# Half of the column table computed and the rest mirrored on Pool, the leftover products of four row tiles put together, and the row statistics of a spectral block moved ahead

## The chip, the core and the metric

The kernel runs on one core of one Trainium2 chip. The metric is the device time of one execution in microseconds (us). A core has five engines with an instruction queue each: TensorE (PE, matrix products; PEld is its weight load), VectorE (DVE), ScalarE (ACT), GpSimd (POOL), and SyncE (SP), which here only issues DMAs. Each queue runs in program order; engines wait for one another by semaphores. Matrix products are written to PSUM, everything else lies in SBUF, in tiles of 128 partitions.

## What is computed

The input x has 2048 rows of 576 numbers in bf16. The first block adds a spectral filter of the normalised rows, the second a gated feed-forward part:

```python
def _A_ref(x, w_r, w_i):
    B, S, D = x.shape
    X = (lambda x, axes=(-2,-1): jnp.fft.rfft2(x.astype(jnp.float32), axes=axes))(x, axes=(-2, -1))
    W = w_r + 1j * w_i
    X = X * W
    y = (lambda x, s, axes=(-2,-1): jnp.fft.irfft2(x, s=s, axes=axes).astype(jnp.bfloat16))(X, (S, D), axes=(-2, -1))
    return y
def _B_ref(x, w_gate, w_up, w_down):
    return (_gelu(x @ w_gate) * (x @ w_up)) @ w_down
x = A_x
h = x + _A_ref(_layernorm(x, axis=-1), A_w_r, A_w_i)
h2 = h + _B_ref(_layernorm(h, axis=-1), B_w_gate, B_w_up, B_w_down)
```

The transform runs over 2048 rows and 576 columns; of the columns 289 frequencies are kept (J, padded to JP = 290). The gate and up weights are 576 x 4608, the down weight 4608 x 576.

## The kernel before

All transforms are matrix products with tables of sines and cosines. Row p * 16 + h of x lies in partition p, so there are sixteen row tiles h of 128 rows each. The program order of every engine is written out by hand (a manual schedule): what stands first in the code is first in that engine's queue.

**First stage** (lines 81 to 451). x comes in six DMAs, then the first halves of the filter WR and WI (line 154). POOL writes index patterns (`iota`, line 172) and the products `kd` from which the column phases come (lines 198 and 199). The first factor of the row transform, the table F16, comes from a sine on ACT (`fs`, line 209) times a mask (`row_table`, line 272). For each row tile the statistics are made either on DVE (`sd`: two `bn_stats` of half a row and one `bn_aggr`, lines 116 to 118; the even tiles and tile 15) or on ACT (`ln_act`, line 123: two passes with an accumulator, the other tiles, finished by `ln_fin` on POOL, lines 127 and 128). POOL then makes 1/sqrt of four tiles at once (`ln_rstd`, lines 132 and 133). DVE normalises each tile into xn (line 136), and PE multiplies it by F16: `row16` (line 288) takes the columns 0 to 255 and 288 to 543 of a tile in four products (line 298, PSUM tile f2t, two row tiles in one), `row16_rest` (line 308) the leftover 64-column pieces in two small ones (line 311, PSUM tile f4, four row tiles in one). Before some tiles `fill` (line 283) gives PE products that nobody reads. `evict` (line 319) and `evict4` (line 327) copy these results to Bt in SBUF, on ACT but for the last f4, which DVE copies. All PSUM tiles here come from one ring of four buffers (`two`, line 66), so the fifth tile waits for the release of the first.

Besides, this stage makes the tables of the later stages. The column table DT (three tiles of 128 columns of x by 2 parities a by cosine or sine r by 145 frequencies) comes from `phases` (line 266, DVE), `drop_sign` and two sines on ACT (`col_sin`, line 346). DF is a copy of a part of DT with zeros elsewhere (lines 387, 429, 430), and DQ a rearrangement of it, which thirteen DMAs on SP make (line 421). The row twiddles TF, nine frequencies k by (minus sine, cosine, sine) by 128, come from `angle_a`, `angle_b`, `angle_c` on DVE (lines 234 to 250), `sine` and `cosine` on ACT and `minus_sine` on DVE (line 258). They are made in two portions, `first` (the first two k in the order of use, 1 and 2) and `rest` (the other seven). `turn_tf` (line 261) makes the transposed copy TI of each portion with one transposing DMA on SP. G16 is a transposed F16 for the way back (line 437 on PE, line 445 on ACT). The second halves of WR and WI are mirrored rows, fetched by two indirect DMAs on POOL (line 381) and put in place by two DMAs on SP (line 411).

SP's queue in this part is: x, WR and WI, their second halves, `turn_tf(first)`, the thirteen DQ copies, `turn_tf(rest)`, then the first weights of the feed-forward part (`load_gu`, line 145, and line 693).

**Frequency stage** (lines 465 to 718). For each k in the order 1, 2, ..., 7, 0, spread over rounds i of one loop (line 668): `f2` multiplies Bt by the column table for k and k + 8 (line 479; `f2_out`, line 490, evicts), `f3` combines them with TF (lines 496 and 497), `sum_of` (line 529) and `wmul` (lines 547 to 571) on DVE form sums and multiply by the filter into Zt, and `i3` goes back over the rows with TI (line 587, one round later; k = 1 is turned in round 3, k = 3 in round 5). Then `inv_cols` (line 638) goes back over the columns with DQ, and `add_rows` (line 770) finishes the first block with G16.

**Feed-forward stage** (from line 850): products with the gate and up weights (line 898), gelu on ACT (line 906), the product on DVE (line 907), and the down product (line 941) with the sums and stores.

The functions that the change touches, with the numbers of the profile:

Of the kernel before, what the change touches and what calls it, by code (L numbers as in the profile page):

```python
# [20 lines left out]
P = 128  # L21
S = 2048
H = 16
D = 576
# [7 lines left out]
NDT = 5  # L32
JW = 58
# [8 lines left out]
def kernel_body(  # L42
# [143 lines left out]
    iota(q16[:], [[16, P]])  # L186
# [4 lines left out]
    iJ = tmp("iJ", [P, JP], FP32)  # L191
# [3 lines left out]
    pd, kd = tmp("pd", [P, 3, JP], FP32), tmp("kd", [P, 3, JP], FP32)  # L195
# [5 lines left out]
    iota(rev[:], [[0, 1]], 2 * P - 1, -2)  # L201

# [9 lines left out]
    ia, s2a, s2p = tmp("ia", [P, 1]), tmp("s2a", [P, 1], FP32), tmp("s2p", [P, 1], FP32)  # L212
    V.tensor_scalar(ia[:], ip[:], 7, None, op0=ALU.bitwise_and)
    V.tensor_scalar(s2a[:], ia[:], 127.0 / 8.0, None, op0=ALU.mult)
    V.scalar_tensor_tensor(s2p[:], ip[:], 0.125, s2a[:], op0=ALU.mult, op1=ALU.add)
    ks = tmp("ks", [P, 9], FP32)
    V.tensor_scalar(ks[:], kv[:], s2p[:, 0:1], None, op0=ALU.mult)
    V.tensor_scalar(iu[:], iu[:], 7, None, op0=ALU.bitwise_and)
    mask = tmp("mask", [P, P], FP32)
    V.tensor_scalar(mask[:], iu[:].rearrange("p c l -> p (c l)"), 0.0, None, op0=ALU.is_equal)  # L220
# [24 lines left out]
    def angle_b(sl):  # L245
        V.tensor_scalar(pr[:, sl], pr[:, sl], 2047, None, op0=ALU.bitwise_and)
        V.tensor_scalar(ab[:, sl], pr[:, sl], -1024.0, None, op0=ALU.add)
# [24 lines left out]
    def row_table():  # L272
        V.tensor_tensor(
            F16[:, 0:2, :],
            fs[:].unsqueeze(1).to_broadcast([P, 2, P]),
            mask[:].unsqueeze(1).to_broadcast([P, 2, P]),
            ALU.mult,
        )
        V.tensor_scalar(F16[:, 2, :], F16[:, 0, :], -1.0, None, op0=ALU.mult)
# [8 lines left out]
    def row16(h):  # L288
        if h % 2 == 0 or h == H - 1:
            ps_f[h] = two("f2t")  # L290
        if h % 4 == 0:
            ps_f["f4", h] = two("f4")
        f2t, b = (ps_f[h], 0) if h in ps_f else (ps_f[h - 1], 1)
        fill(f2t[:, b, :], {0: 14, 8: 8, 12: 5}.get(h, 0))
# [10 lines left out]
        if h < 12:  # L305
            row16_rest(h)
# [12 lines left out]
    def evict(*hs):  # L319
        for h in hs:  # L320
            n = 1 if h >= H - 2 else 2
            A.copy(  # L322
# [9 lines left out]

    def sd(*hs):
        for h in hs:
            ln_dve(mv, h)
# [6 lines left out]
    wm = [tmp(n, [P, 8 * J], BF16) for n in ("wm_r", "wm_i")]  # L342
    xn_pool = tc.tile_pool(name="xn", bufs=1, side="right")
    xn = xn_pool.__enter__().tile([P, H, D], BF16, name="xn")

    def col_sin(r, src, bias):
# [4 lines left out]
            bias=bias[:],  # L351
            scale=-2.0 * PI / D,
        )

    first, rest = slice(0, 2), slice(2, 9)
    ln_act(1)
    ln_act(3)
# [662 lines left out]
```

## Time and profile before

| | us |
|---|---|
| time, median of 3 runs (lowest, highest) | 497.41 (497.33, 497.72) |
| the profiled execution's own time | 497.44 |
| its span, first to last instruction | 495.7 |
| PE busy | 487.6 |
| first stage, to the first product of line 479 | 25.2 |
| first product of the feed-forward stage, line 898 | 68.1 |

The 1.7 us between the span and the time of the profiled execution lie outside its first and last instruction. A row of a timeline reads: start, length, engine, line, operation, output <- inputs with their shapes, count, and in brackets the idle time ahead of it and what ended it. Several instructions of one kind are merged into one row. The chain of waits is followed back from the last instruction; its rows give start, length, and engine, tile and line. SPq is SP's queue, with the time that issuing a DMA took. In the DMA view "under 512 B" counts the packets below that size.

### The profile page before, as it was taken

Reading aid. Unit: us, or ns where it says so; the run is one execution under the profiler, and the core shown is the slowest. Engines: PE = TensorE matmul, PEld = TensorE weight load, DVE = VectorE, ACT = ScalarE, POOL = GpSimd, SP = SyncE. Lnnn points to the kernel's source line nnn. Section 1 sums busy time; section 2 is a strip of 40 time slices with the busy share of each in tenths; the row PEclk is TensorE's granted clock in tenths of the full one; section 3 lists DMA queues with packets and bytes.
Section 4 is the critical chain, followed back from the end, with each engine's and each line's share of the span. In section 5 each row is a group of like instructions: output and inputs, shape, how many; then the busy total and the mean of one; then the engine's idle time right before and its main releaser. Section 6 shows DMA issues by size and latency. Waiting matters only on the chain.

```text
span 495.7 us, 12763 instructions
## 1 busy us (share of the span) xinstructions
PE 487.6 (98%) x5714; PEld 337.6 (68%) x5716; DVE 224.9 (45%) x443; ACT 161.6 (33%) x289; POOL 29.3 (6%) x78
## 2 busy tenths in 40 slices
PE   6999999999999999999999999999999999999997
PEld 3478789885579965555599855555799655555995
DVE  8999884698632157433311244333221333333111
ACT  8999873322211022323300123223110233232000
POOL 8500010011110001000000000000000000000000
PEclk9999999999999999999999999999999999999999
DMA  8739779969990039988730079977700288870000
GB/s 291 214 52 201 207 148 207 185 107 211 213 210 4 3 84 180 209 166 153 145 73 3 1 177 187 199 153 147 144 3 1 79 156 158 156 149 2 13 15 24
DMA packets 89549, 62.33 MB, mean 126 GB/s; under 512 B 23190, under 2 KB 88086, under 8 KB 89494
## 3 DMA queue, kind: packets, MB, share of 16 engines
q1 hardware_dynamic: 89206, 60.34, 61.5%
q0 software_dynamic: 288, 1.18, 0.8%
q8 instruction: 44, 0.72, 0.7%
q14 instruction: 11, 0.09, 0.1%
HBM read 52.65 MB, written 2.36 MB: 111 GB/s over the span
## 4 chain that ended last, share of the span: by engine, by line
PE 95%; POOL 2%; DVE 1%; ACT 1%; issue 0%; POOLq 0%
PE gu L898 57%; PE acc L941 27%; PE pq_ps L479 2%; PE cs_ps L638 2%; PE acc L960 2%; PE eo_ps L587 2%; PE y_ps L770 1%; PE gh_ps L497 1%; PE gh_ps L496 1%; DVE xn L136 1%; POOL rstd L133 0%; PE f2t L298 0%; ACT DT L347 0%; ACT Bt L322 0%; POOL kd L198 0%
## 5 line engine op out<-in xcount | busy, mean ns | idle before, releaser
L898 PE MATMUL gu<-Bt,wgu 64*128 64x512 bf16 (+1 forms) x2646 | 270.6, 363 | 0.0
L898 PEld LDWEIGHTS <-wgu 64*128 64x128 bf16 x2646 | 151.8, 94 | 115.3 <-issue 0.3
L907 DVE TENSOR_TENSOR P_sb<-g_sb,gu 128x512 bf16<-128x512 f32 (+1 forms) x156 | 100.4, 645 | 140.3 <-ACT g_sb L906 140.3
L906 ACT ACTIVATE g_sb<-gu 128x512 f32<-128x512 f32 (+1 forms) x156 | 88.0, 564 | 193.5 <-PE gu L898 193.5
L941 PEld LDWEIGHTS <-P_sb 64*128 64x128 bf16 x2160 | 122.2, 94 | 10.9
L941 PE MATMUL acc<-wd,P_sb 64*128 64x288 bf16 x1440 | 90.9, 283 | 0.0
L950 DVE TENSOR_TENSOR part<-part,acc 128x576 f32<-128x576 f32 x15 | 11.3, 755 | 112.6 <-ACT part L949 112.6
L949 ACT COPY part<-acc 128x576 f32<-128x576 f32 x15 | 9.6, 640 | 122.8 <-PE acc L941 122.8
L941 PE MATMUL acc<-wd_a,P_sb 64*128 64x288 bf16 x720 | 46.8, 283 | 0.0
L898 PE MATMUL gu<-Bt,wgu_e 64*128 64x256 bf16 (+1 forms) x162 | 12.5, 305 | 0.0
L795 DVE TENSOR_SCALAR hrow<-h_sb,mv,rstd 128x1152 bf16<-128x1152 bf16 x14 | 12.2, 868 | 0.6 <-POOL rstd L833 0.6
L479 PE MATMUL pq_ps<-DT,Bt 128*128 128x290 bf16 x64 | 12.3, 286 | 0.0
L286 PE MATMUL f2t<-h_sb,ident 128*128 128x512 bf16 x26 | 8.3, 473 | 3.9 <-DMA h_sb<-in_A_x_dram 3.9
L133 POOL TENSOR_TENSOR rstd<-rstd,mhalf 128x1 f32<-128x1 f32 (+1 forms) x16 | 11.7, 729 | 1.3
L952 DVE TENSOR_TENSOR h_sb<-h_sb,part 128x576 bf16<-128x576 bf16 x15 | 11.4, 758 | 0.5
L898 PEld LDWEIGHTS <-wgu_e 64*128 64x128 bf16 x162 | 10.4, 94 | 1.1
L479 PEld LDWEIGHTS <-Bt 128*128 128x128 bf16 x96 | 9.2, 97 | 2.5
L132 POOL TENSOR_SCALAR rstd<-mv 128x1 f32<-128x1 f32 (+1 forms) x16 | 4.0, 247 | 116.4 <-DVE mv L118 116.1
L638 PE MATMUL cs_ps<-DQ,EO 58*128 58x290 bf16 x144 | 10.8, 283 | 0.0
L490 ACT CAST pq<-pq_ps 128x580 bf16<-128x580 f32 x15 | 9.9, 663 | 0.2
L298 PE MATMUL f2t<-F,xn 128*128 128x256 bf16 x64 | 9.3, 275 | 0.6 <-DVE xn L136 0.6
L123 ACT ACTIVATE junk<-h_sb 128x576 bf16<-128x576 bf16 x14 | 9.4, 674 | 0.6 <-DMA h_sb<-in_A_x_dram 0.6
(138 smaller groups left out, 280.0 us busy)
## 6 DMA issues: line engine op xcount, KB each, us to landing
wgu<-in_B_w_gate_dram SPq DMA_DIRECT2D x46, 432.0 KB
wgu<-in_B_w_up_dram SPq DMA_DIRECT2D x46, 432.0 KB
wd_a<-in_B_w_down_dram SPq DMA_DIRECT2D x1, 1728.0 KB
wd<-in_B_w_down_dram SPq DMA_DIRECT2D x1, 1728.0 KB
wd<-in_B_w_down_dram SPq DMA_DIRECT2D x6, 288.0 KB
out_dram<-h_sb SPq DMA_DIRECT2D x3, 576.0 KB
h_sb<-in_A_x_dram SPq DMA_DIRECT2D x4, 288.0 KB
h_sb<-in_A_x_dram SPq DMA_DIRECT2D x2, 576.0 KB
```

What stands on the lines that cost most here:

```text
L133: G.tensor_tensor(dst[:, sl], dst[:, sl], mhalf[:, sl], ALU.pow)
L479: T.matmul(ps[:, par, 0:JP], lhsT=Bt[:, t, col], rhs=DT[:, t // 2, par] if t < 4 else DF[:, par], start=(t == par), stop=(t == 4),)
L587: T.matmul(pv[:, n], lhsT=z[:, a, w].rearrange("p b j -> p (b j)"), rhs=TI[:, ts[k], 1 - a : 3 - a, :], start=(a == 0), stop=(a == 1),)
L638: T.matmul(ps[:, e, 0:JP], lhsT=EO[x][rows, w, 2 * g : 2 * g + 2].rearrange("p h e k l -> p (h e k l)"), rhs=DQ[rows, w] if w or e else DT ...
L795: V.tensor_scalar(hrow[:], h_sb[:, h, :].rearrange("p (r k) -> p r k", k=64).unsqueeze(2).to_broadcast([P, NR, 2, 64]), mv2[:, h, 0:1], rs ...
L898: T.matmul(gu[:, c, 0:n], lhsT=w[rows, r, i * P : (i + 1) * P], rhs=hl[tcnk % 2][rows, r, lo:hi], start=(r == 0), stop=(r == NR - 1),)
L906: A.activation(g_sb, gu[:, 0, 0:n], ACT.Gelu_apprx_tanh)
L907: V.tensor_tensor(p_sb(f)[:, lo:hi], g_sb, gu[:, 1, 0:n], ALU.mult)
L941: T.matmul(accs[i][:, c, 0:DH], lhsT=p_sb(f)[rows, st * P : (st + 1) * P], rhs=wd[f // NWA][rows, f % NWA, c * DH : (c + 1) * DH], start=( ...
L950: V.tensor_tensor(part, part, accs[1][:, :, 0:DH], ALU.add)
L952: V.tensor_tensor(hv, hv, part, ALU.add)
L960: T.matmul(acc[:, 0, 0:DH], lhsT=p_sb(f)[:, st * P : (st + 1) * P], rhs=wd[f // NWA][:, f % NWA, cc], start=(f == 0), stop=(f == NFT - 1),)
```

## The change

- **Column table.** The phases and both sines are made for 73 of the 145 frequencies only (JM = 73, so iJ, pd and kd have 146 columns in place of 290). A new function `mirror(r)` fills the rest on POOL: one `tensor_scalar` for each parity a reads the computed 72 values backwards, multiplies them by a sign that depends on whether the partition is odd (`sgn`), and writes 3 x 72 elements. The last column of one parity is zeroed by a small memset. `mirror(1)` and `mirror(0)` stand on POOL between the statistics' steps.
- **Leftover products.** `row16_rest` of a group of four row tiles is done in one go behind the group's `row16` products (`rests`), not tile by tile. The PSUM tile f4 is taken then, not at the group's first tile. Fill counts go from 14, 8, 5 to 12, 8, 2.
- **Statistics.** In `sd` the `bn_aggr` of a tile is held back until the first `bn_stats` of the next tile has been issued (`flush` issues one that is left). Tiles 10, 12, 14 and 15 have all of theirs ahead of the normalisation of tiles 8 to 11; before, tile 15 stood behind it.
- **Order.** `phases` and `col_sin(1)` stand before the first normalisation, `drop_sign` and `col_sin(0)` soon after it. The two gathers stand around the rstd of tiles 4 to 7, before it and after it; they stood behind it. DF's memset goes to the start. The steps of TF's portion `first` behind `angle_a` (angle_b, the new `angle_s`, angle_c, sine, cosine, minus_sine) go behind the last evictions; `sine(rest)` goes behind the second `f2`. Issued on SP, `turn_tf(first)` keeps its place behind the second halves of WR and WI and ahead of the DQ copies.
- **Engines.** Row tile 14 is evicted by DVE; the negative half of G16 is made on DVE from the positive one.
- **Small.** The row table's mask is folded into one `scalar_tensor_tensor`; s2p is computed another way, with q16 and ks scaled to match.

The core of the diff:

```diff
-    iota(iJ[:], [[1, 2], [2, JH]])
+    iota(iJ[:], [[1, 2], [2, JM]])
...
+    G.memset(DF[:], 0.0)
+    G.memset(DT[:, :, 1, :, JH - 1], 0.0)
...
+    for r, s in ((0, -2.0), (1, 2.0)):
+        V.tensor_scalar(sgn[:, r : r + 1], odd[:], s, -0.5 * s, op0=ALU.mult, op1=ALU.add)
...
     def angle_b(sl):
         V.tensor_scalar(pr[:, sl], pr[:, sl], 2047, None, op0=ALU.bitwise_and)
+
+    def angle_s(sl):
         V.tensor_scalar(ab[:, sl], pr[:, sl], -1024.0, None, op0=ALU.add)
...
-        fill(f2t[:, b, :], {0: 14, 8: 8, 12: 5}.get(h, 0))
+        fill(f2t[:, b, :], {0: 12, 8: 8, 12: 2}.get(h, 0))
...
+    def rests(h):
+        ps_f["f4", h] = two("f4")
+        for i in range(4):
+            row16_rest(h + i)
...
-            A.copy(
+            (V.tensor_copy if h == 14 else A.copy)(
...
+            V.bn_stats(st[:, 0, :], h_sb[:, h, 0:DH])
+            flush()
+            V.bn_stats(st[:, 1, :], h_sb[:, h, DH:D])
+            agg.append((h, st))
...
-            DT[:, :, :, r, :],
+            DT[:, :, :, r, 0:JM],
...
+    def mirror(r):
+
+        for a in range(2):
+            G.tensor_scalar(
+                DT[:, :, a, r, JM - a : JH - a], DT[:, :, a, r, JM - 2 :: -1], sgn[:, r : r + 1], None, op0=ALU.mult
+            )
```

The order from the statistics to the tables, as it stands after the change:

```python
    for h in (1, 3, 5, 7, 9):
        ln_act(h)
    sd(0)
    V.tensor_scalar(ks[:], kv[:], s2p[:, 0:1], 0.125, op0=ALU.mult, op1=ALU.mult)
    row_table()
    sd(2)
    minus_row()
    sd(4)
    ln_fin(slice(1, 4, 2))
    ln_rstd(rstd, mv, 0, 4)
    sd(6)
    flush()
    phases()
    col_sin(1, pd, zerob)
    norms(0, 4)
    drop_sign(kd[:], pd[:])
    rests(0)
    gather(0)
    ln_fin(slice(5, 8, 2))
    ln_rstd(rstd, mv, 4, 8)
    gather(1)
    evict(0)
    ln_act(11)
    col_sin(0, kd, hpib)
    evict(2)
    evict4(0)
    ln_act(13)
    angle_a(first)
    sd(8)
    norms(4, 8)
    rests(4)
    evict(4)
    mirror(1)
    sd(10, 12)
    ln_fin(slice(9, 12, 2))
    ln_rstd(rstd, mv, 8, 12)
    mirror(0)
    sd(14, 15)
    flush()
    evict(6)
    evict4(4)
    ln_fin(slice(13, 14))
    ln_rstd(rstd, mv, 12, 16)
    norms(8, 12)
    rests(8)
    angle_a(rest)
    evict(8, 10)
    evict4(8)
    norms(12, 16)
    rests(12)
    evict(12)
    V.tensor_copy(DF[0:32], D3[0:32])
    V.tensor_copy(DF[96:128], D3[96:128])
    angle_b(rest)
    angle_b(first)
    evict(14, 15)
    angle_s(first)
    evict4(12)
    angle_c(first)
    angle_s(rest)
    sine(first)
    cosine(first)
    minus_sine(first)
```

Behind it come Zt's memsets, the two DMAs of line 411, `turn_tf(first)`, the halving of two columns of WR and WI on POOL (line 413), the DQ copies, and G16. In round 0 of the frequency stage:

```diff
             angle_c(rest)
+            sine(rest)
             cosine(rest)
...
             minus_sine(rest)
+            V.tensor_scalar(G16v[1], G16v[0], -1.0, None, op0=ALU.mult)
```

More of the change, by code (lines that the diff above doesn't have):

```diff
@@ L412, in kernel_body @@
     for w in (WR, WI):
         G.tensor_scalar(w[:, :, 0 : J : J - 1], w[:, :, 0 : J : J - 1], 0.5, None, op0=ALU.mult)
-    turn_tf(first)
     for r in (1, 0):
@@ L423, in kernel_body @@
                     )
-    for h in range(12, 16):
-        row16_rest(h)
-    evict(12, 14, 15)
-    angle_a(rest)
-    V.tensor_copy(DF[0:32], D3[0:32])
-    V.tensor_copy(DF[96:128], D3[96:128])
-    evict4(12)
-    angle_b(rest)
     pt = two("pt")
```

115 lines of the change are left out of this document (53 added, 62 removed).

## The prediction

> **What bounds the kernel now.** I read the page first, then the chain of waits in order of time, then each engine's timeline over the first 45 us, and the DMA queue's own.
>
> ```profile
> PE 487.6 (98%) x5714; PEld 337.6 (68%) x5716; DVE 224.9 (45%) x443; ACT 161.6 (33%) x289; POOL 29.3 (6%) x78
> PE 95%; POOL 2%; DVE 1%; ACT 1%; issue 0%; POOLq 0%
> 11.54 1.45 DVE xn L136 x4
> 21.28 1.95 ACT DT L347 x2
> 25.22 2.34 PE pq_ps L479 x18
> ```
>
> The reader is to see that PE owns 95% of the chain, and that the rest lies before 25.2 us: the chain runs over POOL (rstd), DVE (statistics, xn) and ACT (column table, evictions of Bt) until the first column product at line 479, and then stays on PE. The change works only ahead of that point and at its edge, so it can win or lose a microsecond or two, and only if what follows lets it.
>
> What follows:
>
> ```profile
> 34.28 1.25 PE L587 MATMUL eo_ps<-TI,Zt 128*128 128x256 bf16 x10
> 41.45 1.25 PE L587 MATMUL eo_ps<-TI,Zt 128*128 128x256 bf16 x10
> 28.89 1.43 DVE L529 TENSOR_TENSOR xab<-g,gh_ps 128x578 bf16<-128x578 bf16 x2 [0.74 <-ACT g L518]
> 33.72 0.45 DVE L568 TENSOR_TENSOR Zt<-zb,za 128x580 bf16<-128x580 bf16 x1
> 37.29 0.45 DVE L568 TENSOR_TENSOR Zt<-zb,za 128x580 bf16<-128x580 bf16 x1
> ```
>
> PE and DVE run one frequency in the same time: PE's line 587 stands two rounds apart in these rows, 7.17 us or 3.58 a round, and DVE's line 568 one round, 3.57. PE starts line 587 0.11 us after DVE ends Zt (33.72 + 0.45). So an earlier start of PE alone is worth nothing: DVE must start its sums (28.89) earlier too. Call what they gain G.
>
> There is a third party, and it decides my forecast: TI, the transposed table that line 587 reads. Two DMAs write it: one for k = 1 and 2, one for the other seven. Line 587 needs the second from its third round on, at 41.45.
>
> ```profile
> 22.44 0.22 DVE L259 TENSOR_SCALAR TF<-TF 128x256 bf16<-128x256 bf16 x1
> 22.72 1.32 SPq L262 DMA_TRANSPOSE TI<-TF  x1
> 24.14 9.87 SPq L421 DMA_DIRECT2D DQ<-DT  x13
> 34.12 3.62 SPq L262 DMA_TRANSPOSE TI<-TF  x1
> DMA packets 450, 0.12 MB, mean 246 GB/s; under 512 B 419, under 2 KB 450, under 8 KB 450
> DMA packets 51, 0.04 MB, mean 78 GB/s; under 512 B 0, under 2 KB 51, under 8 KB 51
> ```
>
> On SP the first transposing DMA starts 0.06 us after minus_sine(first) ends (22.44 + 0.22); thirteen DQ copies follow without a gap, 0.76 each; the second transpose comes right behind. The last two rows are the DMA view of 39.0 to 39.5 and of 39.5 to 40.0: the small packets, the transpose's, end by 39.5. With its completion I take 39.8 as the landing (bounds 39.5 and 41.4). So the second table lands about 17.1 us after the first transpose starts, whatever else happens, and there is 1.65 us of slack. If the first transpose slides by S, and PE starts 0.05 after a landing, **change of time = the larger of -G and S - 1.6**.
>
> **The change part by part.** The order of SP's queue is unchanged; what moves is minus_sine(first). Before, sine, cosine and minus_sine of `first` are done in the middle of the rows; now they come behind the last evictions. So S is the time at which DVE, in its new order, gets to minus_sine(first). I add it up.
>
> ```profile
> 3.87 0.46 DVE L116 BATCH_NORM_STATS2 st<-h_sb 128x6 f32<-128x288 bf16 x1
> 13.88 0.41 DVE L116 BATCH_NORM_STATS2 st<-h_sb 128x6 f32<-128x288 bf16 x1
> 14.20 0.44 DVE L117 BATCH_NORM_STATS2 st<-h_sb 128x6 f32<-128x288 bf16 x1
> 14.67 0.21 DVE L118 BATCH_NORM_AGGREGATE mv<-st 128x2 f32<-128x12 f32 x1
> 14.80 0.41 DVE L116 BATCH_NORM_STATS2 st<-h_sb 128x6 f32<-128x288 bf16 x1
> 18.94 1.33 DVE L268 SCALAR_TENSOR_TENSOR pd<-iJ,iD,kd 128x290 f32<-128x290 f32 x3
> 24.40 0.69 DVE L328 CAST Bt<-f 128x512 bf16<-128x512 f32 x1
> 22.57 1.14 DVE L236 SCALAR_TENSOR_TENSOR pr<-q,s2p,ks 128x896 int32<-128x896 f32 x1
> 23.94 0.43 DVE L430 COPY DF<-DT 32x580 bf16<-32x580 bf16 x1
> 25.12 0.63 DVE L246 TENSOR_SCALAR pr<-pr 128x896 int32<-128x896 int32 x1
> 10.51 0.29 DVE L246 TENSOR_SCALAR pr<-pr 128x256 int32<-128x256 int32 x1
> ```
>
> (a) Statistics. One row takes 0.92 (13.88 to 14.80): 0.32, then 0.47 because the aggregate waits for the second half, then 0.13. The deferred aggregate fills that wait: 0.33 + 0.13 + 0.33 = 0.79. A next instruction starts some 0.07 before the end that a row shows, and each price below is the row less that. DVE starts at 3.87 in both kernels, since both wait for the same x. (b) Up to the phases: four rows 3.2, a bubble at the flush 0.1, row table, its minus and ks 0.8, phases at half width. 1.33 for three of 290 columns is 0.44 each; 146 columns at about one a ns less give 0.29, so 0.87. That is 8.8. rstd of rows 0 to 3 is there at 8.6, as before (it waits for the same ACT sums); xn 0 to 3 take 1.37 (the chain's 1.45 less the last one's tail): 10.2; drop_sign at 438 columns 0.32, between the two rows of line 246; angle_a(first) 0.48, under half of line 236's 896 columns plus its fixed part; row 8's statistics 0.7: 11.7.
>
> Now DVE needs rstd of rows 4 to 7 from POOL.
>
> ```profile
> 6.68 0.18 POOL L127 TENSOR_TENSOR sq<-mv 128x2 f32<-128x2 f32 x1
> 7.54 1.05 POOL L133 TENSOR_TENSOR rstd<-rstd,mhalf 128x4 f32<-128x4 f32 x1
> 10.26 1.24 POOL L133 TENSOR_TENSOR rstd<-rstd,mhalf 128x4 f32<-128x4 f32 x1
> 19.58 1.38 POOL L133 TENSOR_TENSOR rstd<-rstd,mhalf 128x4 f32<-128x4 f32 x1
> 3.90 1.70 POOL L198 TENSOR_SCALAR kd<-iJ,iDs 128x290 f32<-128x290 f32 x3
> 5.68 0.93 POOL L199 TENSOR_SCALAR kd<-kd 128x870 f32<-128x870 f32 x1
> 11.59 1.25 POOL L381 DMA_INDIRECT wm_r<-in_A_w_r_dram,rev  x1
> 14.09 0.60 POOL L387 MEMSET DF<- 128x580 bf16 x1
> ```
>
> (c) POOL. A chain of four small instructions to an rstd takes 1.91 undisturbed (6.68 to 7.54 + 1.05). Its last one takes 1.05 while DVE does statistics, and 1.24 and 1.38 while DVE does angles or phases. The setup: kd at half width saves 1.70 + 0.93 - 1.6 = 1.0 and the moved memset of DF with DT's last column costs 0.7, so POOL still waits at 6.6 for ACT: free of charge, and without that cover up to 0.7. The first gather now stands ahead of the rstd of rows 4 to 7: 8.6 + 1.25 = 9.85, plus 1.9 to 2.6 gives 11.75 to 12.45; I take 12.05. Everything of DVE behind xn 4 waits for it, 0.35. (d) xn 4 to 7: 13.5. Four more rows at 0.79 and the flush: 16.85. xn 8 to 11: 18.2. angle_a(rest) 1.07 (line 236): 19.3.
>
> (e) The mirror. The trace has no such instruction. Four of 3 x 72 elements; the nearest rows are 290 elements in 0.57 and 870 in 0.93, which put 216 at about 0.53; below it cannot be cheaper than the 0.18 of a tiny one, and above I allow 0.93. I take 0.57, near the 290. POOL: 12.05, second gather 13.35, mirror(1) 14.5, rstd of 8 to 11 16.45 (DVE comes at 16.85, no wait), mirror(0) 17.6, rstd of 12 to 15 in 1.9 to 2.8 beside xn 8 to 11 and angle_a(rest): 19.5 to 20.4, I take 20.1. DVE waits 0.8.
>
> (f) xn 12 to 15: 21.5. DF copies 0.7, two of at most the 0.43: 22.2. angle_b of both 0.78 (0.56 and 0.22): 23.0. Row 14's eviction, now DVE's, 0.66, by line 328 (0.69, same elements, also from PSUM): 23.65. angle_s(first) 0.22, evict4(12) 0.66, angle_c(first) 0.22, angle_s(rest) 0.56, minus_sine 0.22: 25.5. First transpose 25.55, **S = 2.8, so +1.2 us**.
>
> ```profile
> 17.09 0.61 PE L298 MATMUL f2t<-F,xn 128*128 128x256 bf16 x4 [0.29 <-DVE xn L136]
> 17.81 0.61 PE L298 MATMUL f2t<-F,xn 128*128 128x256 bf16 x4
> 21.56 1.92 PE L298 MATMUL f2t<-F,xn 128*128 128x256 bf16 x16 [0.34 <-DVE xn L136]
> 23.12 1.98 ACT L322 CAST Bt<-f2t 128x1024 bf16<-128x1024 f32 x3
> 25.26 0.66 ACT L445 ACTIVATE G<-pt 128x256 bf16<-128x256 f32 x2 [0.16 <-PE pt L437]
> ```
>
> (g) PE and ACT. Four rows with leftovers between them take 2.9 (0.72 each); sixteen products in a row 1.85, plus eight leftovers 0.4. That saves PE 0.6 for each of three groups, but PE waits for xn each time (the releaser in the rows is DVE), so it is worth nothing alone. ACT loses half of two table sines (half of the chain's 1.95, less a fixed part: 0.75), row 14 (half an eviction, 0.5), one G (half of 0.66), and sine and cosine of `first` go behind its last eviction: it ends row 15 near 23.2, 0.6 after that row's product (20.1 + 0.45 for xn + 1.85 + 0.2), instead of at 25.1, and then waits for angle_c(first) at 24.8. The first column product (25.22 in the chain) starts near 23.8, behind leftovers and fills. DVE's sums start at about 28.6: from 24.8 on ACT has cosine(first), G, pq, sine(rest), cosine(rest) and g ahead of them, six pieces of 0.3 to 1.0, 3.7 in all. So G is 0.3, and up to 1.3 if POOL never holds DVE. It is lost anyway, since the third round waits for TI. Behind TI everything is PE's own pace, so the wait stays in the end time.
>
> Other moves at nothing: the gathers run 1 to 3 us earlier, hence WR and WI too, long ahead of their use; the DQ copies and the weight loads slide by S, and both are first used behind the whole frequency stage. The early fills, two fewer, leave PE idle for about one us ahead of row 0, which waits for xn.
>
> **A rule against the change.** Rows of line 133: 1.05 alone, 1.24 and 1.38 beside DVE. The Trainium skill, GPSIMD Engine Reference, section 1, Specifications, says that POOL's SBUF interface is shared with VectorE, with contention from instructions in a 2-port mode or with two SBUF inputs; by that rule the mirrors and the last rstd, which lie beside xn and angle_a, cost more than alone, and the trace agrees by 0.2 to 0.3 us each. In its section 3.1 it gives 2.6 cycles an element at 1.2 GHz; by that, an estimate, 216 elements take 0.47 beside the fixed part, 0.7 in all, and my sum would be +1.7.
>
> **Rivals.** R1, the train on SP is harmless: minus_sine(first) ends before 24.2, S is below 1.6, TI lands ahead, and the change is S - 1.6 down to -G. If POOL never holds DVE (0.35 and 0.8 less) it ends at 24.35; with 0.2 to 0.5 off the pitches S is 1.4 to 1.1, and the time 497.2 to 496.9. For it: in the old timeline DVE never waits 0.4 us for POOL. Against: the old POOL had no gather and no mirrors ahead of its rstds. To gain over 1.0 us S must stay below 0.6, minus_sine at 23.2, a full us below the sum without any wait, and G must reach 1.0 as well.
>
> R2, POOL becomes the bound: mirrors at the upper end of 0.93, shut out by DVE. Four times 0.36 more lie ahead of rstd 12 to 15, of which DVE had waited for all: 1.4 more, rstd 21.5, S 4.2: +2.6, 500.0. It counts from a mirror price of about 0.4 on, below which DVE arrives last.
>
> R3, the half table saves nothing, because the strided sine costs as before: ACT has 1.2 us of idle ahead of cosine(first), so 0.75 more would be swallowed: also +1.2.
>
> **How the numbers follow.** The profiled execution is 497.44 us with a span of 495.7; the median shown is 497.41, the same. 497.4 + 1.2 = 498.6. The sum's own range is S from 1.6 (no POOL wait at all) to 3.7, +0 to +2.1. Chances: forecast with R3 0.60, R1 0.22, R2 0.18. The range goes from 497.1 (part of R1) to 500.0 (most of R2). A measurement here tells 0.2%, 1.0 us, from no change; +1.2 lies just over that. Of the forecast's 0.60 I give 0.34 to over 1.0, of R2 all 0.18; of R1 0.09 to faster by over 1.0, the rest to within: faster 0.09, same 0.39, slower 0.52.
>
> **What would show it.** Right: the first TI transpose on SP at 25 to 26 instead of 22.72 with the thirteen copies still 0.76 apart; line 587's third round with a wait for the DMA; line 479 starting near 23.8; DVE idle ahead of xn 4 and xn 12 with POOL's line 133 as releaser; a mirror at 0.5 to 0.7. Wrong: line 587 going on every 3.57 without a wait, or the transpose before 24.3, which is R1; DVE held over 1.5 us before xn 12, which is R2. The forecast fails altogether if the second transpose takes another length from the first than 17.1, or if PE, once held, makes up time later because DVE has run ahead.

## The result, and the profile after

The changed kernel took 500.09 us (median of 5 runs, 500.02 to 500.20), the kernel before on the same chip 497.54 (497.33 to 498.19). The ratio is 1.005 with an interval of 1.0035 to 1.0064: slower by 2.55 us, where 1.2 was forecast and 500.0 was the end of the range. The profiled execution took 500.09 us, its span is 498.3; before, 497.44 and 495.7.

Where the time goes is seen by following the first stage from its end. PE's timeline of the changed kernel first, its first column product and its third round:

```profile
26.66 0.67 PE L514 MATMUL pq_ps<-DT,Bt 128*128 128x290 bf16 x4
39.62 1.25 PE L622 MATMUL eo_ps<-TI,Zt 128*128 128x256 bf16 x10
44.11 1.25 PE L622 MATMUL eo_ps<-TI,Zt 128*128 128x256 bf16 x10 [0.77 <-DMA TI<-TF]
47.67 1.25 PE L622 MATMUL eo_ps<-TI,Zt 128*128 128x256 bf16 x10
```

The third round starts at 44.11 in place of 41.45, 2.66 later, and 2.65 is what the profiled execution lost. It waits for the second transposing DMA (TI), and behind it the rounds follow at 3.56 as before. SP's timeline shows why the table is late:

```profile
27.37 1.32 SPq L266 DMA_TRANSPOSE TI<-TF  x1
28.79 9.87 SPq L470 DMA_DIRECT2D DQ<-DT  x13
38.77 3.23 SPq L266 DMA_TRANSPOSE TI<-TF  x1
```

The same train of DMAs, started 4.65 us later (22.72 before). Its start waits for VectorE's minus_sine, and VectorE's timeline shows two waits for POOL ahead of that:

```profile
12.33 2.16 DVE L137 TENSOR_SCALAR xn<-h_sb,mv,rstd 128x576 bf16<-128x576 bf16 x4 [0.82 <-POOL rstd L134]
22.01 1.65 DVE L137 TENSOR_SCALAR xn<-h_sb,mv,rstd 128x576 bf16<-128x576 bf16 x4 [1.53 <-POOL rstd L134]
27.09 0.21 DVE L263 TENSOR_SCALAR TF<-TF 128x256 bf16<-128x256 bf16 x1
30.70 1.43 DVE L564 TENSOR_TENSOR xab<-g,gh_ps 128x578 bf16<-128x578 bf16 x2 [0.91 <-ACT g L553]
```

In the kernel before, row 12 came without a wait:

```profile
21.00 1.52 DVE L136 TENSOR_SCALAR xn<-h_sb,mv,rstd 128x576 bf16<-128x576 bf16 x4
```

So row 12 is normalised 1.01 later, behind 1.53 of idling, and VectorE's first sums start at 30.70 (28.89). Two things are late: the sums by 1.81, and the transposed table, for which the third round waits, so that it starts 2.66 late. The later one counts. POOL, for which both wait, has this timeline:

```profile
8.50 1.38 POOL L367 DMA_INDIRECT wm_r<-in_A_w_r_dram,rev  x1 [0.21 <-issue]
...
11.24 1.05 POOL L134 TENSOR_TENSOR rstd<-rstd,mhalf 128x4 f32<-128x4 f32 x1
12.48 1.24 POOL L367 DMA_INDIRECT wm_i<-in_A_w_i_dram,rev  x1 [0.19 <-issue]
13.78 1.77 POOL L389 TENSOR_SCALAR DT<-DT,sgn 128x216 bf16<-128x216 bf16 x2
...
16.39 1.04 POOL L134 TENSOR_TENSOR rstd<-rstd,mhalf 128x4 f32<-128x4 f32 x1
17.44 1.83 POOL L389 TENSOR_SCALAR DT<-DT,sgn 128x216 bf16<-128x216 bf16 x2
19.24 0.23 POOL L128 TENSOR_TENSOR sq<-mv 128x1 f32<-128x1 f32 x1
19.55 0.98 POOL L129 TENSOR_TENSOR mv<-mv,sq 128x1 f32<-128x1 f32 x1
20.62 0.23 POOL L133 TENSOR_SCALAR rstd<-mv 128x4 f32<-128x4 f32 x1
20.94 1.04 POOL L134 TENSOR_TENSOR rstd<-rstd,mhalf 128x4 f32<-128x4 f32 x1
```

From 8.5 to 22 POOL hardly rests, and the four mirrors (line 389) are 3.6 us of it, 0.9 each. The view by windows makes the exchange plain. Of the stretch from 8.5 to 22.0 it gives the busy time of PE, PEld, DVE, ACT and POOL (then the granted clock, the share of the DMA engines and GB/s); before:

```profile
8.50:22.00 13.50, 12.80 (x91) 6.63 (x91) 12.91 (x38) 13.18 (x28) 9.64 (x20) 1.00 0.92 274
```

and after the change:

```profile
8.50:22.00 13.50, 9.65 (x84) 5.77 (x82) 11.13 (x31) 12.74 (x25) 12.45 (x19) 1.00 0.92 278
```

VectorE lost 1.8 us of work, POOL gained 2.8. VectorE, with 0.6 of its 13.5 idle before, now idles for 2.4, while POOL has 1.1 left of 3.9.

### The profile page after: what moved, and what is told of

Read it like the earlier page. It is cut to its first block, busy times and chain, and to the rows that moved or that the text cites. A ratio compares the mean times of both kernels' runs of the same rounds, so it can differ in the third digit from the quotient of the medians.

```text
span 498.3 us, 12760 instructions
## 1 busy us (share of the span) xinstructions
PE 485.4 (97%) x5711; PEld 336.8 (68%) x5711; DVE 224.1 (45%) x445; ACT 160.2 (32%) x287; POOL 32.5 (7%) x83
## 4 chain that ended last, share of the span: by engine, by line
PE 92%; ACT 3%; DMA 2%; POOL 1%; DVE 1%; issue 1%; POOLq 0%
PE gu L935 56%; PE acc L978 27%; PE cs_ps L673 2%; PE acc L997 2%; ACT junk L124 2%; PE eo_ps L622 1%; PE pq_ps L514 1%; DMA TI<-TF 1%; PE y_ps L807 1%; PE gh_ps L532 1%; DMA h_sb<-in_A_x_dram 1%; PE gh_ps L531 1%; ACT Bt L331 0%; POOL DT L389 0%; ACT pq L525 0%
## 5 line engine op out<-in xcount | busy, mean ns | idle before, releaser
L304 PE MATMUL f2t<-F,xn 128*128 128x256 bf16 x64 | 7.9, 274 | 4.5 <-DVE xn L137 4.5
L304 PEld LDWEIGHTS <-xn 128*128 128x128 bf16 x64 | 5.7, 98 | 7.4 <-DVE xn L137 6.6
```

The source lines that it names most:

```text
L304: T.matmul(f2t[:, b, t * 2 * P : (t + 1) * 2 * P], lhsT=x[:, d0 : d0 + P], rhs=F16[:, n : n + 2, :], start=(n == 0), stop=(n == 1),)
```

## The experiments

**Theory A**: the end of the kernel follows the later of two events, the first sums and the second transposed table. Both hang on POOL's last reciprocal root (of rows 12 to 15), which POOL reaches late because of the mirrors. **Theory B**: POOL is not it; VectorE's own new order, the transposes, or the half table itself cost the time. The form that B takes, and a theory C where there is one, stand in each expectation. Each result is the median, with the interval of its ratio to the kernel before.

### Is it POOL's mirrors?

```diff
-            G.tensor_scalar(
+            V.tensor_scalar(
                 DT[:, :, a, r, JM - a : JH - a], DT[:, :, a, r, JM - 2 :: -1], sgn[:, r : r + 1], None, op0=ALU.mult
```

> The changed kernel with one edit: the four mirror instructions are VectorE's instead of POOL's, at the same places of the program. Theory A (POOL's mirrors, 0.82 to 0.98 each, hold the root of rows 12 to 15): VectorE takes four instructions more, some 0.2 each by its pass over 256 elements of bf16 (0.21), so 0.8 in all, but its wait of 1.53 ahead of row 12 goes; row 12 is normalised near 20.9 instead of 22.01, the first transpose is issued near 26.2 instead of 27.37: 499.0 us (498.6 to 499.4). Theory B (VectorE is the bound, and POOL's mirrors were hidden by it): 500.5 to 501.0, later by the four instructions. If a pass that reads backwards costs VectorE as much as it costs POOL (0.9 each), row 12 comes at 21.9 or later and the time stays near 500.

498.22 us (1.0013; 1.0004 to 1.0022): of 2.55 us 1.87 come back. VectorE's timeline of this run shows two mirrors and row 12, without a wait:

```profile
13.79 0.51 DVE L389 TENSOR_SCALAR DT<-DT,sgn 128x216 bf16<-128x216 bf16 x2
20.39 1.44 DVE L137 TENSOR_SCALAR xn<-h_sb,mv,rstd 128x576 bf16<-128x576 bf16 x4
```

A mirror costs VectorE a quarter of a us. Row 12 comes 1.62 sooner, more than expected: rows 4 to 7 also went faster (1.49, not 2.16). In PE's timeline 0.73 of waiting for TI is left:

```profile
42.31 1.25 PE L622 MATMUL eo_ps<-TI,Zt 128*128 128x256 bf16 x10 [0.73 <-DMA TI<-TF]
```

Next the suspected cost is raised: `mirror(0)` issued twice on POOL.

```diff
     mirror(0)
+    mirror(0)
```

> The changed kernel with the second pair of mirrors issued twice on POOL, the same values written again. Theory A (POOL's queue is the bound of the first stage, so that each us put on it ahead of the root of rows 12 to 15 comes out at the end): the pair took 1.83, so row 12 is normalised near 23.8 instead of 22.01, the first transpose is issued near 29.2, third round near 45.9: 501.9 us (501.6 to 502.2). Theory B (VectorE or the transposes bound, POOL has room): 500.1 to 500.6.

501.86 us (1.0088; 1.0074 to 1.0102), as A has it: one more pair of mirrors on POOL, and the end is 1.8 later. In the profiled execution the way there is not quite A's. The last root starts only 1.44 later (22.38). The other 0.4 comes from PE: it idled for 2.3 us, its granted clock was 0.50 from 24.8 to 28.2, the sixteen products of rows 12 to 15 took 2.92 in place of 1.92, and VectorE's last eviction waited for PE:

```profile
24.06 2.92 PE L304 MATMUL f2t<-F,xn 128*128 128x256 bf16 x16 [2.31 <-DVE xn L137]
```

Is it POOL's order or its sum? Both gathers behind the root of rows 4 to 7:

```diff
-    gather(0)
     ln_fin(slice(5, 8, 2))
     ln_rstd(rstd, mv, 4, 8)
+    gather(0)
     gather(1)
```

> The changed kernel with one edit: POOL issues the first gather behind the reciprocal root of rows 4 to 7 (both gathers then stand there, one behind the other) instead of ahead of it. Theory A (the end follows the larger of two delays, that of the first sums of VectorE and that of the first transposing DMA, and both follow POOL's reciprocal root of rows 12 to 15, which POOL reaches late for all that stands ahead of it): rows 4 to 7 get their root near 10.4 instead of 12.3, VectorE's wait of 0.82 ahead of normalising row 4 is gone, POOL's mirrors are over 0.5 to 0.8 sooner, the first transpose is issued near 26.6 instead of 27.37: 499.3 us (499.1 to 499.6). Theory B (POOL's gathers are harmless, only the mirrors count, and the two mirrors are where they were): 500.1. If the two gathers beside VectorE's normalising of rows 4 to 7 slow it to more than the 2.16 of four that it took, the gain is smaller by so much: 499.6 to 500.1.

500.45 us (1.0046 to 1.0074): a miss for A as it was put. Rows 4 to 7 did get their root a us sooner and VectorE's first wait went (one of 0.69 ahead of row 8 came in its place), but the last root started where it had, as POOL's timeline shows:

```profile
10.22 1.07 POOL L134 TENSOR_TENSOR rstd<-rstd,mhalf 128x4 f32<-128x4 f32 x1
...
20.95 1.04 POOL L134 TENSOR_TENSOR rstd<-rstd,mhalf 128x4 f32<-128x4 f32 x1
```

The last root waits for all that stands ahead of it, in this order too. So A is narrowed: it is POOL's sum of work ahead of the last root that counts.

### Two ends: the sums and the transposed table

The second transposing DMA ahead of the thirteen copies (`dq_copies` holds line 470 with its loops):

```diff
                     turn_tf(rest)
+                    dq_copies()
```

> The changed kernel with one thing moved: on SP the second transpose of TF stands ahead of the thirteen DQ copies instead of behind them. Theory A (the time is the later of two things, DVE's first sums, 1.81 us late at 30.70 against 28.89, and TI's second landing, 2.66 us late for line 622 at 44.11 against 41.45): the wait for TI goes, and the sums' 1.81 is left, so 499.3 us, 0.8 below the changed kernel. Theory B (only the late first stage costs, and PE would lose the 0.8 elsewhere): 500.1, no change. Theory C (TI is the whole loss): 497.5 or less.

499.16 us (1.0020 to 1.0045). PE no longer waits for TI; what is left is the 1.7 by which the sums are late. The other way to free the table is to start the train early, with the twiddles of `first` taken from behind the last evictions to behind `angle_a(first)`, and minus_sine to behind `flush`:

```diff
     angle_a(first)
+    angle_b(first)
+    angle_s(first)
+    angle_c(first)
+    sine(first)
+    cosine(first)
     sd(8)
...
     flush()
+    minus_sine(first)
```

> The changed kernel with angle_b, angle_s, angle_c, sine, cosine and minus_sine of the first portion back among the row tiles, ahead of the third group. Theory A: minus_sine(first) ends near 18, the first transpose starts right behind the second halves of WR and WI, near 18.3, TI is never late; DVE has 0.75 us less behind xn 12 to 15 and PE's first column product comes about 0.3 earlier, so the sums are 1.5 late instead of 1.8: 499.0 us. Theory B (position of the tables is indifferent): 500.1. Theory C (TI is the whole loss): 497.5.

498.95 us (1.0019 to 1.0044), with the first transpose at 18.06, and again the late sums are left. The same SP edit together with the mirrors on VectorE takes away both:

> The changed kernel with two edits: the mirrors on VectorE, and the second transposing DMA ahead of the 13 copies on SP. With the mirrors alone moved it was at 498.2, its first sums at 28.93 (28.89 before) and its third round of products at 42.31 (41.45 before), which waited 0.73 for the second transpose. Theory A (the end follows the later of the two, and the wait for the transpose is all that is left): 497.5 us (497.3 to 497.8), third round near 41.5 without a wait. Theory C (something further down in the kernel is slower by the change): 498.0 to 498.3.

497.60 us (0.9991 to 1.0009): the old time, third round at 41.38 without a wait. And the SP edit alone in the kernel before:

> The kernel before with one edit: SP issues the second transposing DMA ahead of the 13 copies of the column table instead of behind them. Theory A (in the kernel before the train on SP is over 1.65 us before TensorE asks for its result, so its length does not count): no change, 497.5 us (497.3 to 497.8). Theory C (the train costs something in the kernel before too, and what the changed kernel gave away by it is more than its slide less 1.6): 496.5 to 497.0. If the column table's copies, now later by some 3 us, were needed sooner than that: slower, 498 and more.

497.71 us (0.9993 to 1.0011): no change. In the old kernel the train's length was free; the change spent its slack.

### The other parts

The whole column table as before, no mirrors (the index and phase tiles at full width, `DT[:, :, :, r, :]`, DF's memset in the mirror's place):

> The changed kernel with the whole column table computed again (146 columns back to 290, no mirrors on POOL, the memset of DF between the statistics where the first mirrors stood); all the rest of the change stays. Theory A (the four mirrors of 0.82 to 0.98 on POOL hold the statistics of the last group and through them everything behind): the rstd of tiles 12 to 15 near 19.3 instead of 21.98, xn 12 near 19.5, minus_sine(first) near 24.8, TI 0.1 late, the sums 0.7 earlier than in the kernel before: 497.6 us. Theory B (the grouped leftover products and the waiting PE cost the time): about 500. Theory C (sine on ACT was the limit, so the halving helped): above 500.1.

498.78 us (1.0014 to 1.0034), a miss of 1.2. POOL's last root did start at 19.12 and row 12 did not wait, but VectorE was the limit: with the wider phases row 0 came at 9.63 (8.65), row 12 at 20.93, and with all its twiddles behind the rows the first transpose at 26.16. TI was late by 0.65, the sums by 0.60. With the SP edit on top:

> The changed kernel with the whole column table computed as before the change (no mirrors), and the second transposing DMA ahead of the 13 copies on SP. With the whole table alone it was at 498.78, its first sums at 29.49 and its third round waiting 0.65 for the transpose. Theory A (the end follows the later of the first sums and the transpose; half a table with mirrors on VectorE saves VectorE some 0.5): the wait goes, the sums stay, 498.1 us (497.9 to 498.3), against the 497.6 of the half table with the same order on SP. Theory B (half the table saves nothing on balance): 497.6, like it. If the wait for the transpose was not what set the end: 498.8.

497.98 us (0.9999 to 1.0017), as A has it. Against the half table with mirrors on VectorE (497.60) that is 0.4; the two intervals overlap, but the third rounds, 41.97 and 41.38, point the same way.

The second pair of mirrors behind the last root on POOL:

```diff
     ln_rstd(rstd, mv, 8, 12)
-    mirror(0)
...
     ln_rstd(rstd, mv, 12, 16)
+    mirror(0)
```

> The changed kernel with one step moved on POOL: the second pair of mirrors stands behind the last rstd instead of ahead of it. Theory A: the last rstd comes about 1.8 us earlier, xn 12 near 20.45, minus_sine(first) near 25.8, TI 1.1 late and the sums 0.3 late: 498.6 us, 1.5 below the changed kernel. Theory B (POOL's total counts, not its order, since DF's copies wait for the mirrors): 500.1.

499.17 us (1.0020 to 1.0044), half right: row 12 at 20.39, as expected, but VectorE's copies to DF now waited for the mirrors. The two took 2.66, as the first began in VectorE's pass over the angles (19.62, pass from 19.32 to 20.47) and took 1.81.

The grouped leftovers alone, in the kernel before (`rests` as in the change, nothing else):

> The kernel before with one part of the change: the leftover products of four tiles are issued together behind the four tiles' main products. Prediction's step (the grouping alone is worth nothing, since VectorE's and ScalarE's work sets when rows 12 to 15 are ready): 497.5 us (497.2 to 497.8). Rival (TensorE's queue counts in the first stage, and fewer changes between the two shapes bring the rows' products forward by up to the 0.1 to 0.3 that PE waited for normalised rows): 497.0 to 497.2. If the evictions, which now wait for four leftovers at once, are late by it: 498 or more.

497.30 us (0.9988 to 1.0006): no difference that can be measured.

### What makes a mirror dear

Forms that nobody reads, on POOL behind its last memset, where it has no other work (`scr`, `scf` are scratch; the mirrors are on VectorE). First type, direction and scalar, over 3 x 72 elements:

```diff
+    for _ in range(3):
+        G.tensor_scalar(scr[:, :, 1:73], DT[:, :, 0, 0, JM - 2 :: -1], sgn[:, 0:1], None, op0=ALU.mult)
+        G.tensor_scalar(scr[:, :, 0:72], DT[:, :, 0, 0, 0 : JM - 1], sgn[:, 0:1], None, op0=ALU.mult)
+        G.tensor_scalar(scr[:, :, 0:72], DT[:, :, 0, 0, 0 : JM - 1], -1.0, None, op0=ALU.mult)
+        G.tensor_scalar(scf[:], DT[:, :, 0, 0, 0 : JM - 1], sgn[:, 0:1], None, op0=ALU.mult)
+        G.tensor_scalar(scf[:], pd[:, :, 0 : JM - 1], sgn[:, 0:1], None, op0=ALU.mult)
```

> The changed kernel with the mirrors on VectorE, and fifteen instructions more on POOL behind its last memset of the stage (three rounds of five forms over 3 x 72 elements, into scratch tiles that nobody reads): backward bf16 to bf16 at an odd offset with a scalar per partition (the mirror's form), the same forward at an even offset, forward with an immediate, forward bf16 to float32, float32 to float32. They stand where POOL has no other work until 67 us, so the time should stay within 1 us of 498.2; what is read is what each costs. If reading backward is what made the mirror cost 0.82 to 0.98: the first form takes 0.8 or more, the other four 0.4 to 0.6. If the type or the three short runs are it: the first three or four forms take about the same 0.8 to 0.9, and only float32 from float32 0.4 to 0.5. If it is the time shared with VectorE: each form's least time is 0.4 to 0.6, and each form spreads widely.

In POOL's timeline the least times of the five forms are 0.82, 0.82, 0.75, 0.82 and 0.83: direction and type are not it. (The time, 505.58, was a miss: a step of ACT waited for the last scratch tile.) So the three separate runs were the suspect, and were tried as one run, one run backward, three and six:

```diff
+        G.tensor_scalar(flat, line[:, 0:216], sgn[:, 0:1], None, op0=ALU.mult)
+        G.tensor_scalar(flat, line[:, 215::-1], sgn[:, 0:1], None, op0=ALU.mult)
+        G.tensor_scalar(scr[:], DT[:, :, 0, 0, 0:72], sgn[:, 0:1], None, op0=ALU.mult)
+        G.tensor_scalar(sc6[:], DT[:, :, :, 0, 0:36], sgn[:, 0:1], None, op0=ALU.mult)
```

> The changed kernel with the mirrors on VectorE and twelve instructions more on POOL behind its last memset of the stage (three rounds of four forms, each with a scalar per partition, into scratch tiles that nobody reads; as their memory is used again later, the kernel's time is late by them and isn't read): 216 elements as one run, the same run backward, as three runs of 72, as six runs of 36. If the price goes by separate runs: near 0.45 for one run (worked out from POOL's 0.40 for 146 contiguous elements and 0.61 for 438), near 0.82 for three as before, near 1.2 for six. If it goes by instruction and element alone: 0.8 for all four. If backward costs, but only in one long run: the second form stands out.

That suspect falls too. POOL's timeline has all four forms alike, each by its least time:

```profile
23.42 0.83 POOL L497 TENSOR_SCALAR scr<-DT,sgn 128x216 bf16<-128x216 bf16 x1
24.35 0.83 POOL L498 TENSOR_SCALAR scr<-DT,sgn 128x216 bf16<-128x216 bf16 x1
...
29.44 0.82 POOL L499 TENSOR_SCALAR scr<-DT,sgn 128x216 bf16<-128x216 bf16 x1
30.24 0.83 POOL L500 TENSOR_SCALAR sc<-DT,sgn 128x216 bf16<-128x216 bf16 x1
```

One difference from the rows that the prediction priced by was left: those instructions had two operations (multiply, add), a mirror has one.

```diff
+        G.tensor_scalar(scr[:, 0:72], line[:, 0:72], sgn[:, 0:1], None, op0=ALU.mult)
+        G.tensor_scalar(scr[:], line[:, 0:432], sgn[:, 0:1], None, op0=ALU.mult)
+        G.tensor_scalar(scr[:, 0:216], line[:, 0:216], sgn[:, 0:1], 0.0, op0=ALU.mult, op1=ALU.add)
+        G.tensor_scalar(scf[:], kf[:, 0:216], sgn[:, 0:1], 0.0, op0=ALU.mult, op1=ALU.add)
+        G.tensor_scalar(scr[:, 0:216], line[:, 0:216], -1.0, 0.0, op0=ALU.mult, op1=ALU.add)
```

> The changed kernel with the mirrors on VectorE and ten instructions more on POOL behind its last memset of the stage (two rounds of five forms into scratch tiles that nobody reads; the time isn't read): multiply by a scalar per partition over 72 and over 432 elements of bf16; multiply and add 0.0 over 216 of bf16, over 216 of float32, and with an immediate over 216 of bf16. If the price goes by elements at some 2 ns each (from 0.38 for 34 and 0.75 for 216 with an immediate): near 0.5 for 72, 1.3 for 432, and 0.8 for all three of 216. If the one-operation form is the dear one: the three forms with two operations take 0.4 to 0.5. If the price is the same up to some size: 0.82 for 72 too.

POOL's timeline, of each form the shorter of its two:

```profile
23.50 0.47 POOL L497 TENSOR_SCALAR scr<-DT,sgn 128x72 bf16<-128x72 bf16 x1
...
26.67 0.44 POOL L500 TENSOR_SCALAR scf<-kd,sgn 128x216 f32<-128x216 f32 x1
27.09 0.36 POOL L501 TENSOR_SCALAR scr<-DT 128x216 bf16<-128x216 bf16 x1
...
28.27 1.36 POOL L498 TENSOR_SCALAR scr<-DT,sgn 128x432 bf16<-128x432 bf16 x1
29.72 0.45 POOL L499 TENSOR_SCALAR scr<-DT,sgn 128x216 bf16<-128x216 bf16 x1
```

(The times of these two kernels, 498.52 and 498.62 in one execution each, hold the scratch work and say nothing of the mirrors.) With one operation the time grows by 0.89 us from 72 to 432 elements, 2.5 ns an element; with two, 216 elements take 0.45, where one takes 0.82. Why is open. But the second operation, adding 0.0, should make the mirrors cheaper:

```diff
-                ... sgn[:, r : r + 1], None, op0=ALU.mult
+                ... sgn[:, r : r + 1], 0.0, op0=ALU.mult, op1=ALU.add
```

> The changed kernel with one edit: each of the four mirrors, still on POOL, has a second operation that adds 0.0 (multiply and add in one instruction), as POOL's rows at 0.40 for 146 elements and 0.61 for 438 have two operations. If the one-operation form is what costs 0.82 to 0.98: a mirror takes about 0.45, 1.8 less in all stands ahead of the root of rows 12 to 15, and the time is 498.3 to 498.7. If the price hangs on the elements alone, whatever the operations: 500.1, or more by what the second operation costs.

498.30 us (1.0016; 1.0007 to 1.0025): 1.8 us less than the changed kernel, by an instruction that does more. POOL's groups by line give four mirrors, their sum and the mean in ns, in the changed kernel

```profile
L389 POOL TENSOR_SCALAR DT<-DT,sgn 128x216 bf16<-128x216 bf16 x4 | 3.6, 905 | 0.1
```

and with the second operation

```profile
L389 POOL TENSOR_SCALAR DT<-DT,sgn 128x216 bf16<-128x216 bf16 x4 | 1.8, 456 | 0.1
```

### A version faster than both?

Mirrors on VectorE, both gathers behind the root of rows 4 to 7, twiddles early as above, and VectorE's two evictions first:

```diff
+    evict(14, 15)
+    evict4(12)
     angle_b(rest)
-    evict(14, 15)
-    evict4(12)
```

> The changed kernel with four edits that each take away one named delay: the mirrors on VectorE instead of POOL, both gathers behind the root of rows 4 to 7, the first twiddles (angle, sine, cosine, minus sine of the first two) back among the row tiles, and VectorE's evictions of row 14 and of the four leftovers ahead of its pass over the angles of the rest. Theory A (POOL's root of rows 12 to 15 and the serial tail behind it are all that makes the changed kernel slower; the half table and the grouped leftovers do save VectorE, TensorE and ScalarE time): row 12 is normalised near 20.3 (before: 21.00), the first column product comes near 24.1 (25.16), the first sums near 27.9 (28.89), and the transposing DMAs are never late: 496.5 us (496.2 to 497.2), below the kernel before. Theory B (the half table and its mirrors cost as much as they save wherever they stand, so that at best the old time comes back): 497.5 to 498.0. Theory C (what delays is none of the four): 499 and more.

497.46 us (0.9990 to 1.0008), a miss for A. The profiled execution, 496.90, has its third round 0.54 earlier than before, but its eleven executions spread from 496.69 to 498.20, and the median shows no gain; why they spread is open. The same with two-operation mirrors on POOL:

> The changed kernel with the mirrors on POOL in the two-operation form (0.46 each instead of 0.91), both gathers behind the root of rows 4 to 7, the first twiddles back among the row tiles, and VectorE's evictions of row 14 and of the four leftovers ahead of its pass over the angles of the rest. Theory A: row 12 is normalised near 19.7 (before: 21.00; with the mirrors on VectorE 20.46), POOL's last root comes at the same time, the first sums near 27.7 (28.89) and the third round near 40.3 (41.45): 496.3 us (496.0 to 496.8), below the kernel before by more than 0.2%. Theory B (the first stage has another floor that the old kernel was already at): 497.3 to 497.6.

497.30 us (0.9985 to 1.0003): a miss again. POOL's timeline has a reason, and VectorE's beside it:

```profile
18.88 1.78 POOL L134 TENSOR_TENSOR rstd<-rstd,mhalf 128x4 f32<-128x4 f32 x1
```

```profile
18.62 1.14 DVE L238 SCALAR_TENSOR_TENSOR pr<-q,s2p,ks 128x896 int32<-128x896 f32 x1
20.69 1.57 DVE L137 TENSOR_SCALAR xn<-h_sb,mv,rstd 128x576 bf16<-128x576 bf16 x4 [0.93 <-POOL rstd L134]
```

The last root began 0.26 into VectorE's pass over the angles and took 1.78, not 1.05. No version was faster than the kernel before by more than the measurement can tell.

### The sum

The third round's shift against the kernel before (41.45) is the shift of the profiled execution's time (497.44), to 0.05:

| kernel | last root starts | first sums | third round | its shift | time's shift |
|---|---|---|---|---|---|
| changed | 20.94 | 30.70 | 44.11, waits for TI | +2.66 | +2.65 |
| second pair twice (clock 0.50 for 3.4 us) | 22.38 | 32.84 | 45.88 | +4.43 | +4.43 |
| gathers behind | 20.95 | 30.64 | 43.97, waits | +2.52 | +2.53 |
| TI ahead of DQ | 20.87 | 30.62 | 43.10 | +1.65 | +1.70 |
| twiddles early | 20.87 | 30.45 | 42.93 | +1.48 | +1.50 |
| mirrors on VectorE | 18.57 | 28.93 | 42.31, waits | +0.86 | +0.86 |
| two operations | 18.99 | 28.77 | 42.20, waits | +0.75 | +0.73 |
| whole table, TI first | 19.12 | 29.49 | 41.97 | +0.52 | +0.52 |
| on VectorE, TI first | 18.53 | 28.90 | 41.38 | -0.07 | -0.07 |

## Why the prediction missed

**The frame held, one of its constants did not.** The time was to change by the slide S of the first transpose less a slack of 1.6, since the second table was to land 17.1 after the first transpose starts, "whatever else happens". The trace tells of a landing by the DMA's last semaphore update: 39.85 in the kernel before, so the 39.8 of the prediction was right, and 43.97 in the changed one. That is 17.13 and 16.60 after the start; nine more runs in which the train starts late, as in the changed kernel, have 16.5 to 16.6, and the kernel before with grouped leftovers 17.1. Why is open; SP's own time for the second transpose was 3.62 before and 3.23 after. The third round starts 0.14 behind the landing. So the slide was 4.65, the train shorter by 0.53, and from the transpose's start to the third round it is 16.74 (44.11 - 27.37): the slack was in effect 2.0 (41.45 - 22.72 - 16.74), and 4.65 - 2.0 is the 2.65. The shorter train hid part of the miss, by luck. Behind TI, PE kept its own pace, as forecast.

**Steps (a), (b) and (f) held.** A row's statistics took 0.79, the phases 0.88, and from row 12 to the transpose it was 5.36 (5.45 forecast).

**Step (e) failed**, by its size: "I take 0.57, near the 290". The mirrors took 0.91 on average. The two rows behind the 0.57 were of multiply-and-add instructions; a multiply alone is dearer on POOL (0.82 against 0.45 for 216 elements, where POOL has no other work). From the start of a pair to what follows it the mirrors took 1.74 and 1.80, where I had put 1.15 each. That is 1.2 us, of the 1.9 by which the last root was late (21.98 against 20.1). The Trainium skill's rule in the prediction (GPSIMD Engine Reference, section 3.1, 2.6 cycles an element, 0.7 in all) was nearer than my rows: 2.5 ns an element is 3.0 cycles at the 1.2 GHz of its section 1. But that was luck: the section gives the 2.6 for a `tensor_tensor` with two inputs, a mirror has one, and the two-operation form, with one input as well, is below it.

**Steps (c) and (d) were short.** The root of rows 4 to 7 came at 12.29 (12.05), VectorE waited 0.82 (0.35), and normalising rows 4 to 7 took 2.16 (1.37 forecast). Why they took 2.16 is not settled: with the mirrors on VectorE the same gather lay beside them and they took 1.49, but with the whole table, which has no mirrors, 2.18. It did not delay the last root, as POOL had no wait for VectorE behind it. The second gather cost 0.2 more than I put. The last chain on POOL took 2.74 where I took 2.5; line 129 is 0.98 of it, in place of 0.19, which lay inside the 1.9 to 2.8 allowed. The root of rows 4 to 7, the gather and this chain are the other 0.7.

So the last root was ready at 21.98 instead of 20.1, and this is rival R2 by its numbers: mirrors "at the upper end of 0.93", rstd 21.5, S 4.2, 500.0, and by its sign, VectorE held over 1.5 ahead of row 12 (1.53). It had 0.18 of the chances. Its reason, "shut out by DVE", was not the main one: a mirror's form took 0.82 with nothing else on POOL. That its 500.0 fell within 0.1 of the time is luck in part: S was 4.65, and the shorter train took the difference back. The row nearest in elements had been taken without asking whether it was the same operation.

**Step (g) was wrong in sign.** G was to be a gain of 0.3; the sums came 1.81 later. Of this, 1.01 is the late row 12, 0.49 lies between row 12 and the column product (4.65, before 4.16) and 0.31 behind it. The order was against the gain from the start: by my own step (f) VectorE's eviction of the leftovers ends at 24.5, behind the 23.8 at which I let the column product start. With the twiddles early the product came 4.48 behind row 12's start, with the twiddles early and these evictions first 3.94 (24.40 - 20.46). The late sums were hidden behind TI, and became the bound as soon as TI was freed. **R1 and R3:** R1 is out. R3's reason is out too: a sine over the half table took ACT 0.65, over the whole 1.04. What the half table saves with the mirrors on VectorE is some 0.4, which the overlapping intervals leave unproven.

## What to carry to other kernels

Before work is moved to an idle engine, add up all that stands in its queue ahead of the result that others wait for: here POOL seemed idle on average (6% busy before the change), but ahead of its last root it was full, and a different order of the same sum brought nothing. A price is taken from a row with the same operation, not only the same size. Where two late events end in one wait, freeing one shows only the difference to the other.

## What the runs showed of the hardware

- On POOL a `tensor_scalar` with two operations was faster than with one: 0.45 against 0.82 for 216 elements where POOL has no other work; 0.46 against 0.91 in the first stage. Starts of neighbours stand as far apart (0.42 against 0.93), so it is not only how the profile draws a span.
- A mirror costs VectorE 0.25, a quarter to a third of what its one-operation form costs POOL.
- A POOL instruction that started while VectorE ran one with two inputs took longer by most of what was left of that: 0.98 for 0.19 (19.55, VectorE's pass of line 238 from 19.35 to 20.48) and 1.78 for 1.05 (18.88, pass from 18.62 to 19.76). One input on POOL's side is enough: with the twiddles early, line 133 took 1.01 for 0.23 (19.78, pass from 19.56 to 20.70). One that began 0.09 ahead of such a pass took its 1.06 (18.99, pass from 19.08, two-operation mirrors). The Trainium skill, SBUF — State Buffer, section SBUF: two separate sides, says that the pair of ports these engines share is locked by whoever starts first for a whole instruction; the trace agrees where POOL starts second. Where VectorE did, it does not: the pass from 19.08 began while POOL's root had 0.98 to go, and took 1.14, as it did at 22.57 in the kernel before.
